# One attention-and-experts kernel: two latencies of its order's planner raised, and all its offsets chosen anew

## The chip, the cores and the metric

The kernel runs on one core of a Trainium2 chip. The metric is the time of one execution on the device in microseconds (us); of several runs the median counts. A span is the time from the first to the last instruction in a profiled execution.

## The reference, cut to what matters

Attention over 8 batches and 8 heads (576 tokens, head size 64) in which each query keeps only its 32 largest scores, and then a layer of 8 experts in which each token, if a skip score is positive, goes to the one expert with the largest gate value.

```python
scores = scale * np.matmul(q, k.transpose(0, 1, 3, 2))
kth = np.partition(scores, -top_k, axis=-1)[..., -top_k:-top_k + 1]      # top_k = 32
scores = np.where(scores >= kth, scores, -1000000000.0)
scores = scores - np.max(scores, axis=-1, keepdims=True)
attn = np.exp(scores)
attn = attn / (np.sum(attn, axis=-1, keepdims=True) + 1e-09)
out = np.matmul(attn, v)
...
do_compute = x @ w_skip > 0
xc = x[do_compute]
logits = xc @ w_gate
e_idx = np.argmax(logits, axis=1)
...
h = np.maximum(xc[mask] @ w1[e], 0.0)            # for each expert e
y[mask] = gate_w[mask, None] * (h @ w2[e])
out[do_compute] = xc + y
```

## The kernel before, in words

**The attention** works on 32 pairs of heads (p = 0 to 31). Each pair has nine rows of 128 queries (`row`, s = 9p + i). For one row TensorE multiplies queries by keys into one of three PSUM row buffers (L652; a first pass with the high parts QH, a second with the low parts QL), VectorE finds the largest values with MAX8 over seven pieces (L662) and narrows them down (L668, L670), ScalarE copies the row out (`xc`, L704) and marks what lies above a bound (`r`, L684), GpSimd multiplies the two (`xw`, L707), VectorE takes the last eight (`wn`, L728), and ScalarE writes the mask PEN (L725). Behind it `unit` multiplies keys by queries once more with the mask added (L867, L869, L874), ScalarE takes the exponential (PT, L899), and `values` multiplies by V and sums up (f1: L950 and L953; f2: L967 and L969; f3 to f9 divide and make the gate's logits).

**What a new pair needs.** `load` brings q and k in (two times three DMAs, L503 and L504), `prep` turns them on TensorE (L537), ScalarE puts the result into TT (L542, L548), GpSimd splits it into high and low parts (HI L562, LO L565), and ten copies from SBUF to SBUF, issued by SyncE (L570), bring the parts to the partitions where they are needed: KK<-HI, QH<-HI, KK<-LO and last QL<-LO. (Pair 0 is built by compute engines in `first`.) The first row of a pair waits for its copies (`ready`). Each pair also sends its rows' maxima from ScalarE's tile `mt` to QL by six small DMAs on SyncE (`maxes`, L825 and L831), fetches V (L516, L519) and stores its results twice (L366, L367). SyncE issues all of them in one queue in order.

**The order** of all this is not written by hand. `Plan` simulates the five engines at build time. Each task has an engine, a duration, a due value (in rows) and predecessors. It is ready at the end of its predecessors, plus their `lag`, plus a wait `WAIT[(from, to)]` (or `WAIT[from]`). `pick` takes, among tasks that are ready first, the one with the lowest due value; LOOK and GAIN allow a more urgent task that is ready a little later, KEEP holds back tasks that would take the last buffer, and TURN adds to the due value of a TensorE task that needs another tile mode (128 or 32 rows). What comes out is only the order in which instructions stand on each engine; on the chip an instruction starts when its semaphores allow, whatever the plan thought. The due values are sums of offsets in `K` and, by row number or part, in `FINE`. A second, shorter plan orders the first expert of the second stage.

**The second stage** (the experts) gathers the tokens of each expert (L1139), runs both matrix products in high and low parts (L1216 to L1218, L1239 to L1241) and scatters the results (L1146). After the first expert its order is fixed by the program text.

Of the kernel before, what the change touches and what calls it, by code (L numbers as in the profile page):

```python
# [25 lines left out]
SKIP = 32  # L26

ENGS = ("PE", "ACT", "DVE", "POOL", "SP")
WAIT = {"PE": 0.2, "ACT": 0.16, ("ACT", "PE"): 0.25, ("ACT", "ACT"): 0.143, "DVE": 0.128, ("DVE", "PE"): 0.25, ("DVE", "POOL"): 0.155, ("ACT", "POOL"): 0.18, "POOL": 0.08, "SP": 0.0,
        ("PE", "PE"): 0.0}  # L30
LOOK, GAIN, KEEP = 0.162, 6.776, 65.356
DRAIN, TURN = 0.2, 29.341
K = dict(qk=-6.401, cand=-6.272, kt=-2.354, push=-12.895, count=-0.049, window=2.533, kth=6.545, rf=32.928, pen=-26.284, u0=6.388, u1=9.914, av=-0.737, a0=3.034, a1=6.191, a2=1.611, co=46.109, sm=-12.508, ca=47.359, tx=-2.868, rt=10.372, rd=-4.654, rs=1.553, pp=12.331, ps=0.569, mx=14.567, f3=5.146, f4=1.248, f5=-7.942, ex=-27.446, us=-0.174, cs=-61.75, ch=0.082, ce=-10.579, lg=1.796, ld=10.949, hl=7.464, hs=-0.126, moe=13.163)

FINE = dict(qk=(-2.911, -0.549, -4.826, -6.903, 2.442, -2.322, -0.945, -1.333, 0.435), ch=(-2.085, -1.45, -1.043, 0.316, -0.011, -0.071, -0.036, -0.392, 1.828), cand=(-3.963, -0.264, 0.827, -1.958, 0.278, 1.229, -5.247, 6.017, 1.231), tx=(-1.055, 5.715, 10.279, 5.202, -1.628, 2.466, 5.022, 2.391, -4.558), kt=(-3.211, 4.865, 0.885, -3.921, -6.437, 3.663, 0.801, 7.673, -4.021), push=(-2.868, -6.928, -2.311, -3.59, 1.547, -1.812, -2.748, -2.193, -12.477), fill=(5.442, -5.764, -1.132, 2.354, -0.665, 2.454, -9.578, 5.161, -6.534), window=(-0.6, 0.433, 0.108, 0.426, -0.223, 0.294, 1.865, -1.999, -0.659), rf=(-2.93, -1.353, -5.81, -2.188, -5.243, -19.285, 10.019, -0.327, -7.401), u=(0.614, -1.895, 0.986, 0.567, -1.265, -0.247, 2.714, -0.285, -0.442), ex=(-1.701, 3.29, -6.117, 0.828, -6.929, -1.417, -0.587, 1.819, -1.658), f1=(-0.189, -4.164, 1.973, -3.388, 0.648, 0.187, -8.021, -2.877, -0.757, -0.71, 1.828, 0.724, -5.471, -2.811, 2.068), f2=(-2.357, -5.603, 1.057, -0.011, -2.434, 5.392, -1.655, -9.716, 1.806), f3=(-2.128, -0.617, 1.736, 2.344, 0.698, -1.856), f4=(3.878, 1.05, -1.924), f5=(3.406, 10.908, 2.309, -4.457, 9.428, 4.705, 2.484, -1.786, 0.821), pp=(-2.088, 3.917, 0.282), pa=(-4.97, -0.526, 1.742), hl=(-0.737, -0.356, 0.256, -2.249), mx=(-1.191, 4.185, 5.019, 0.427, -11.874, -2.914), sm=(-0.212, 0.442, 7.091, 0.24, -3.598, -4.48))
CA = (1, 3, 6, 7)
OUT = (0, 1, 2, 3, 4, 5, 6, 7, 8)
PD = ()
# [7 lines left out]
def tile_kernel(ctx, tc, q, k, v, w_skip, w_gate, w1, w2, out):  # L46
# [7 lines left out]
    REM = S - NM * P  # L54
    assert REM == 64 and D == 64 and H % 4 == 0
    NR = 2 * NM + 1
# [18 lines left out]
    ld = att.enter_context(tc.tile_pool(name="ld", bufs=2))  # L75
# [199 lines left out]
    pl = Plan()  # L275
# [30 lines left out]
    lg = cp.tile([P, B, KC, E + 1], F32, name="lg")  # L306
# [216 lines left out]
    def prep(p):  # L523
        i = p % NQ
        hi, lo = slice(0, D), slice(D, P)

        old = [ROWQ[s] for s in range(NR * (p - NQ), NR * (p - NQ + 1))] + TU[p - NQ] if p >= NQ else []
        TURNED[0, p], TURNED[1, p] = [], []
        puts = {0: [], 1: []}

        def turn(h, blocks):

            def f():
                pm = h()
                for j, (nm, t) in enumerate(blocks):
                    src = RAW[nm][:, t] if t < NM else RAWR
                    nc.tensor.transpose(pm[:, j * P:(j + 1) * P], src.rearrange("p h d -> p (h d)"), identF)  # L537
            return f

        def put(h, nms):  # L540
            if len(nms) == 1:
                nc.scalar.activation(TT[:, nms[0], REM:S], h.t[:, 0:MAIN], AF.Copy)  # L542
            else:

                a = TT[:, :, 0:REM]
                a = bass.AP(a.tensor, a.offset, [a.ap[0], a.ap[1], [S, 2], a.ap[2]])
                src = h.t[:, 0:P].rearrange("p (n c) -> p n c", n=2)
                nc.scalar.activation(a, src[:, :, None, :].to_broadcast([P, 2, 2, REM]), AF.Copy)  # L548
        groups = [[(0, t) for t in range(NM)], [(0, NM)], [(1, t) for t in range(NM)]]
        for j, g in enumerate(groups):  # L550
            nms = [0, 1] if j == 1 else [g[0][0]]
            h = Hold(BT, 1)
            due = NR * p - K["pp"] + K["ps"] * j
            x = pl.add("PE", 0.11 * len(g), due + FINE["pp"][j], turn(h, g), [LOADED[nm, p] for nm in nms], take=h)
            y = pl.add("ACT", 0.478 if len(g) > 1 else 0.265, due + 0.1 + FINE["pa"][j], lambda h=h, nms=nms: put(h, nms), x,
                       [SPLIT[nm, p - 1] for nm in nms] if p else None, give=[h])
            for nm in nms:
                TURNED[nm, p].append(x)
                puts[nm].append(y)

        def high(nm):
            nc.gpsimd.tensor_copy(HI[:, nm], TT[:, nm])  # L562

        def low(nm):
            nc.gpsimd.tensor_tensor(LO[:, nm], TT[:, nm], HI[:, nm], op=OP.subtract)  # L565

        def copy(dst, src):
            if len(dst.shape) == 3:
                src = src[:, None, :].to_broadcast(list(dst.shape))
            nc.sync.dma_start(dst.bitcast(F32), src.bitcast(F32))  # L570
        COPIED[p] = []
        if p == 0:
            first(puts)
            return
        for nm in range(2):
            due = NR * p - K["hl"] + K["hs"] * nm
            x = pl.add("POOL", 0.73, due + FINE["hl"][2 * nm], lambda nm=nm: high(nm), puts[nm], CFREE.get(nm))
            y = SPLIT[nm, p] = pl.add("POOL", 1.57, due + FINE["hl"][2 * nm + 1], lambda nm=nm: low(nm), x)
            c = []
            for h in range(2):  # L580

                ps, cs, ds = slice(h * D, (h + 1) * D), slice(REM * (1 - h), S + REM * (1 - h)), slice(HB * h, HB * h + S)
                of_hi, of_lo = HI[ps, nm, cs], LO[ps, nm, cs]
                for dst, src, z in ((KK[i][hi, :, ds], of_hi, x), (KH[i][lo, ds], of_lo, y)) if nm == 0 else (
                        (QH[i][hi, ds], of_hi, x), (QH[i][lo, ds], of_hi, x), (QL[i][hi, ds], of_lo, y)):
                    c.append(pl.add("SP", 0.67, NR * p - 3 + h, lambda dst=dst, src=src: copy(dst, src), z, old, lag=2.4))
            CFREE[nm] = c
            COPIED[p] += c
        if old:
            COPIED[p].append(pl.add("SP", 0.67, NR * p - 3, lambda: copy(QL[i][D:D + 2], QL[i][D + 2:D + 4]), old, lag=2.0))  # L590
# [311 lines left out]
    def heads(p):  # L902
# [30 lines left out]
        def values(pair, n, hs, due, at):  # L933

            h = Hold(VB, 2)
            st = {}
            z = n == REM
# [18 lines left out]
            def f2(kcs):  # L956

                for kc in kcs:
                    for u, (a, qs) in enumerate(pair):
                        for t in range(1 if z else n // P):  # L960
                            r0 = 64 * u + 32 * (kc % 2 if z else t)
                            o = h.t[r0:r0 + 32, 256:256 + m]
                            first = kc < SA + (2 if z else 1)
                            cs = slice(qs + t * P, qs + t * P + m)
                            if kc < NM:
                                pt = pts[a][:, kc, cs] if kc > SA or not SA else SUM[2 * p + a][:, cs]
                                nc.tensor.matmul(o, ones, pt, start=first, stop=(kc > NM - 2 and z), tile_position=(0, r0))  # L967
                            else:
                                nc.tensor.matmul(o, oneh[:, a], pr[:, cs], start=first, stop=True, tile_position=(0, r0))  # L969
# [53 lines left out]
            A = pl.add  # L1023
# [6 lines left out]
            us = users[:]  # L1030
            for j in range((NM + 2 - SA) // 2):
                kcs = range(SA + 2 * j, min(SA + 2 * j + 2, KC))
                y = A("PE", 0.45 if n > REM else 0.235, due + K["av"] * (2 + 2 * j) + FINE["f2"][3 * at + j], lambda kcs=kcs: f2(kcs), us[-1],
                      [SUMMED[2 * p + a] for a in hs], mode=32)
                us.append(y)
            due += K["av"] * KC + K["f3"]
# [7 lines left out]
            y = A("DVE", 0.11, due + K["f5"] + FINE["f5"][3 * at + 1], f8, x, LGFREE[-3:-2], give=[h4])  # L1044
# [35 lines left out]
    y = pl.add("SP", 5.0, 18.0, load_gate, x, lag=2.5)  # L1080
# [511 lines left out]
```

## Time and profile before

| what | value |
|---|---|
| median of 3 runs | 1198.71 us (1194.42 to 1203.68) |
| the profiled execution's own time | 1204.32 us |
| its span | 1202.4 us |
| TensorE (PE) busy | 1120.5 us, 93% |
| VectorE (DVE) busy | 998.4 us, 83% |
| ScalarE (ACT) busy | 935.2 us, 78% |
| GpSimd (POOL) busy | 749.0 us, 62% |
| mean granted TensorE clock | 0.973 |

The profile lists how long each engine was busy and what ended each of its idle times. Shares over the whole span mix two stages: the attention, up to about 880 us, and the experts after it. PE's busy time is modelled, so a busy PE may still work slowly; the column PEclk (1.00 is 2.4 GHz, 0.50 is 1.2 GHz) tells when.

### The profile page before, as it was taken

The page shows a single profiled execution, that of the slowest core. Times are in us where ns is not written, and L with a number is a line of the kernel's source. Part 1 is how long each engine was busy: PE and PEld are TensorE (multiplying, and loading weights), DVE is VectorE, ACT ScalarE, POOL GpSimd, SP SyncE. Part 2 cuts the span into 40 slices and gives each one's busy share as a digit, 9 for nine tenths or more (in the row PEclk, how much of TensorE's full clock was granted, in tenths as well). Part 3 has the DMA queues.
Part 4 walks back from the last instruction along what each step waited for, and adds up shares of the span by engine and source line. Part 5 has one row for each costly group of instructions (what it writes and reads, how often), then busy time and mean ns, then how long its engine had stood idle before and what let it go on. Part 6 is the DMA issues. An engine that isn't in the chain of part 4 may idle for free. (4 is left out here: it accounts for less than half of the span.)

```text
span 1202.4 us, 37703 instructions
## 1 busy us (share of the span) xinstructions
PE 1120.5 (93%) x13012; PEld 947.2 (79%) x13012; DVE 998.4 (83%) x5250; ACT 935.2 (78%) x1965; POOL 749.0 (62%) x997
## 2 busy tenths in 40 slices
PE   4899999999999999999999999999988999999996
PEld 3778888778778788888887788877767988888885
DVE  8899999989899899999999999999965655655541
ACT  5899999989899899999998799998962533333320
POOL 7778787767777688777877799877842022222210
PEclk9699999989999999999998899999989999999998
DMA  6445455545454455654545354753056554544300
GB/s 146 94 111 119 112 131 133 131 116 131 114 121 112 112 127 136 146 131 125 121 110 130 82 120 117 165 151 84 22 178 188 164 166 155 162 160 155 113 21 25
DMA packets 197404, 148.42 MB, mean 123 GB/s; under 512 B 100898, under 2 KB 162850, under 8 KB 197204
## 3 DMA queue, kind: packets, MB, share of 16 engines
q1 hardware_dynamic: 190340, 135.54, 44.5%
q0 software_dynamic: 3840, 9.47, 2.3%
q8 instruction: 105, 1.72, 0.6%
q10 hardware_dynamic: 3024, 0.90, 0.3%
q14 instruction: 95, 0.78, 0.2%
HBM read 68.31 MB, written 25.31 MB: 78 GB/s over the span
## 5 line engine op out<-in xcount | busy, mean ns | idle before, releaser
L707 POOL TENSOR_TENSOR xw<-xc,r 128x576 f32<-128x576 f32 x288 | 369.9, 1285 | 158.3 <-ACT r L684 153.9
L662 DVE MAX8 cand<-r 128x8 f32<-128x82 f32 (+1 forms) x2016 | 384.4, 235 | 20.8 <-PE r L652 20.5
L684 ACT ACTIVATE r<-xc,cl 128x576 bf16<-128x576 f32 x288 | 223.6, 777 | 23.4 <-DVE cl L668 19.1
L725 ACT ACTIVATE PEN<-xc,wn 128x576 bf16<-128x576 f32 x288 | 222.5, 774 | 1.8 <-DVE wn L728 1.6
L728 DVE MAX8 wn<-xw 128x8 f32<-128x585 f32 x288 | 216.8, 753 | 0.8 <-POOL xw L707 0.7
L867 PE MATMUL r<-QH,KK 128*128 128x256 f32 (+1 forms) x640 | 190.9, 325 | 5.8 <-ACT PT L899 3.6
L704 ACT ACTIVATE xc<-r 128x576 f32<-128x576 f32 x288 | 184.9, 642 | 8.1 <-DVE cand L662 6.6
L869 PE MATMUL r<-QL,KK 66*128 66x256 f32 (+1 forms) x640 | 175.1, 301 | 0.4 <-DMA QL<-mt 0.4
L652 PE MATMUL r<-KK,QH 128*128 128x288 f32 x640 | 160.7, 342 | 13.2 <-ACT xc L704 5.7
L668 DVE MAX8 cl<-cand 128x8 f32<-128x28 f32 (+2 forms) x864 | 166.6, 193 | 4.4
L899 ACT ACTIVATE PT<-r 128x576 f32<-128x576 f32 x256 | 162.9, 645 | 6.3 <-PE r L874 6.0
L1146 POOL DMA_INDIRECT out_dram<-ot,idx x24 | 24.4, 1018 | 214.4 <-DVE ot L1145 167.2
L652 PE MATMUL r<-KK,QL 66*128 66x288 f32 x640 | 137.8, 306 | 18.2 <-DMA QL<-LO 16.3
L1112 DVE TENSOR_TENSOR lo<-raw,hi 128x1024 fp32r<-128x1024 f32 x64 | 79.1, 1238 | 76.4 <-ACT hi L1109 75.5
L867 PEld LDWEIGHTS r<-QH,KK 128*128 128x128 f32 x640 | 120.5, 194 | 19.5 <-ACT PT L899 7.8
L874 PE MATMUL r<-nbi,PEN 128*128 128x128 bf16 (+1 forms) x1632 | 133.3, 217 | 0.0
L1109 ACT ACTIVATE hi<-raw 128x1024 fp32r<-128x1024 f32 x64 | 67.4, 1055 | 75.9 <-PE py L1241 71.4
L652 PEld LDWEIGHTS r<-KK,QL 66*128 66x128 f32 x640 | 104.9, 196 | 21.3 <-issue 10.8
L869 PEld LDWEIGHTS r<-QL,KK 66*128 66x128 f32 x640 | 120.7, 194 | 0.7 <-issue 0.7
L652 PEld LDWEIGHTS r<-KK,QH 128*128 128x128 f32 x640 | 98.4, 196 | 28.8 <-ACT xc L704 7.7
L670 DVE MATCH_REPLACE8 cand<-cl,cand 128x28 f32<-128x28 f32 x576 | 103.4, 180 | 0.0
L1221 ACT ACTIVATE hh<-ph 128x352 fp32r<-128x352 f32 (+2 forms) x72 | 30.9, 431 | 91.1 <-PE ph L1218 89.3
(256 smaller groups left out, 2574.0 us busy)
## 6 DMA issues: line engine op xcount, KB each, us to landing
raw<-in_moe_w_dram SPq DMA_DIRECT2D x64, 512.0 KB
KK<-HI SPq DMA_DIRECT2D x62, 288.0 KB
QH<-HI SPq DMA_DIRECT2D x124, 144.0 KB
QL<-LO SPq DMA_DIRECT2D x62, 144.0 KB
KK<-LO SPq DMA_DIRECT2D x62, 144.0 KB
raw<-in_k_dram SPq DMA_DIRECT2D x64, 128.0 KB
V<-in_v_dram SPq DMA_DIRECT2D x32, 256.0 KB
raw<-in_q_dram SPq DMA_DIRECT2D x62, 128.0 KB
```

The costliest lines, as they stand in the source:

```text
L652: nc.tensor.matmul(R(u, w), t[0:k0, c:c + P], KH[i2][0:k0, HB * hd + u:HB * hd + w], start=(k0 == P and x == 0), stop=(k0 < P and x == len ...
L662: nc.vector.max(C[s][:, c], R(CH[c], CH[c + 1]))
L668: nc.vector.max(L[:, 4 * r:4 * r + 8], c)
L684: nc.scalar.activation(RR[s], XC[s], AF.Sign, bias=CL[p][:, i, 23:24], scale=-ODD, accum_out=CN[:, s:s + 1])
L704: nc.scalar.activation(XC[s], R(), AF.Copy)
L707: nc.gpsimd.tensor_tensor(xw()[:, 0:S], XC[s], RR[s], op=OP.mult)
L725: nc.scalar.activation(pen, XC[s], AF.Relu, bias=least, scale=-1.0)
L728: nc.vector.max(WN[p][:, i], XW[s] if out_ else R())
L867: nc.tensor.matmul(t, KH[i2][:, ks], QH[i2][:, qs], start=(y == 0), stop=False)
L869: nc.tensor.matmul(t, KO[i2][:, ks], QL[i2][0:D + 2, qs], start=False, stop=False)
L874: nc.tensor.matmul(rb[:, O + c:O + c + z - a], PEN[p][:, PS * i + REM + c0 - o:PS * i + REM + c0 - o + P], nbi[:, a:z], start=False, stop= ...
L899: return pl.add("ACT", 0.535, due + K["ex"] + FINE["ex"][at], lambda: nc.scalar.activation(dst, st["r"], AF.Exp, scale=scale), x, give=[h])
```

## The change

Three things are edited in the planner's inputs; no instruction is added or taken out.

1. `WAIT` gets an entry ("ACT", "SP"): 1.2. Before, SyncE's tasks after ScalarE fell back on `WAIT["ACT"]`, 0.16.
2. The ten copies between partitions in `prep` get lag 3.0 where they had 2.4.
3. The duration of f2's tasks is written as a product with the number of blocks. With SA = 1 there are two blocks in each, so 0.45 stays 0.45, and 0.235 becomes 0.236.
4. LOOK, GAIN, KEEP, TURN and all values of `K` and `FINE` are replaced.

```diff
-WAIT = {"PE": 0.2, "ACT": 0.16, ("ACT", "PE"): 0.25, ("ACT", "ACT"): 0.143, ..., ("ACT", "POOL"): 0.18, "POOL": 0.08, "SP": 0.0,
+WAIT = {"PE": 0.2, "ACT": 0.16, ("ACT", "PE"): 0.25, ("ACT", "ACT"): 0.143, ..., ("ACT", "POOL"): 0.18, ("ACT", "SP"): 1.2, "POOL": 0.08, "SP": 0.0,
-LOOK, GAIN, KEEP = 0.162, 6.776, 65.356
-DRAIN, TURN = 0.2, 29.341
-K = dict(qk=-6.401, cand=-6.272, kt=-2.354, push=-12.895, ..., rf=32.928, ..., sm=-12.508, ..., mx=14.567, ..., cs=-61.75, ..., ld=10.949, hl=7.464, ..., moe=13.163)
+LOOK, GAIN, KEEP = 0.164, 7.176, 67.94
+DRAIN, TURN = 0.2, 39.21
+K = dict(qk=-6.436, cand=-7.822, kt=-6.355, push=-12.756, ..., rf=40.955, ..., sm=-27.744, ..., mx=16.505, ..., cs=-44.193, ..., ld=11.234, hl=6.901, ..., moe=22.067)
-FINE = dict(qk=(-2.911, -0.549, -4.826, ...
+FINE = dict(qk=(-2.582, -5.481, -3.89, ...
...
-                    c.append(pl.add("SP", 0.67, NR * p - 3 + h, lambda dst=dst, src=src: copy(dst, src), z, old, lag=2.4))
+                    c.append(pl.add("SP", 0.67, NR * p - 3 + h, lambda dst=dst, src=src: copy(dst, src), z, old, lag=3.0))
...
-                y = A("PE", 0.45 if n > REM else 0.235, due + K["av"] * (2 + 2 * j) + FINE["f2"][3 * at + j], lambda kcs=kcs: f2(kcs), us[-1],
+                y = A("PE", (0.225 if n > REM else 0.118) * len(kcs), due + K["av"] * (2 + 2 * j) + FINE["f2"][3 * at + j], lambda kcs=kcs: f2(kcs), us[-1],
```

## Rows read from the trace of the kernel before

**Rows 1.** Busy time by stretch, whole span in parts: us, busy us (instructions), clock, DMA

```profile
0.00:40.00 40.00, 20.93 (x90) 17.45 (x91) 35.03 (x172) 26.16 (x51) 30.34 (x70) 0.84 0.58 134
...
880.00:900.00 20.00, 15.82 (x268) 13.49 (x271) 9.25 (x21) 12.60 (x23) 8.88 (x12) 0.86 0.79 251
900.00:1000.00 100.00, 93.55 (x648) 83.60 (x639) 56.70 (x116) 38.93 (x66) 19.97 (x33) 0.99 0.53 170
```

**Rows 2.** The same view, the attention in pieces (columns PE, PEld, DVE, ACT, POOL)

```profile
60.00:228.00 168.00, 161.30 (x2257) 134.26 (x2259) 162.59 (x989) 164.15 (x362) 129.98 (x166) 1.00 0.50 119
228.00:256.00 28.00, 25.36 (x324) 20.52 (x313) 22.88 (x140) 23.76 (x53) 20.23 (x26) 0.88 0.51 118
256.00:284.00 28.00, 27.24 (x390) 22.88 (x392) 27.19 (x167) 27.33 (x61) 20.41 (x26) 1.00 0.50 119
284.00:312.00 28.00, 25.60 (x343) 21.41 (x336) 24.22 (x151) 24.67 (x55) 20.43 (x26) 0.94 0.50 119
312.00:396.00 84.00, 81.71 (x1199) 68.64 (x1198) 81.39 (x500) 82.84 (x185) 66.42 (x83) 1.00 0.53 127
396.00:424.00 28.00, 25.21 (x309) 20.49 (x312) 23.77 (x146) 24.23 (x54) 19.01 (x26) 0.94 0.46 109
424.00:620.00 196.00, 190.53 (x2705) 159.48 (x2698) 191.26 (x1156) 191.54 (x424) 154.20 (x198) 1.00 0.56 134
620.00:676.00 56.00, 52.68 (x646) 43.54 (x649) 52.14 (x286) 46.75 (x101) 38.15 (x48) 0.88 0.47 111
```

**Rows 3.** DVE's and PE's waits, 40 to 880 us: total us, times, longest us

```profile
DVE cand L662 <- PE r L652: 20.5, 24, 2.5
PE r L652 <- DMA QL<-LO: 16.3, 10, 2.8
```

**Rows 4.** DVE's waits again, of the stretches 226:257, 283:311 and 390:420

```profile
DVE cand L662 <- PE r L652: 4.6, 2, 2.5
DVE cand L662 <- PE r L652: 3.3, 2, 1.7
DVE cand L662 <- PE r L652: 3.8, 2, 2.2
```

**Rows 5.** Timeline around 248 us: start us, us, engine line op, idle before

```profile
247.56 1.16 SPq L570 DMA_DIRECT2D QL<-LO  x2
...
249.99 0.85 PE L652 MATMUL r<-KK,QL 66*128 66x288 f32 x2 [2.65 <-DMA QL<-LO]
...
250.77 3.64 PE L950 MATMUL pt<-PT,V 128*32 128x256 f32 x32
250.88 0.25 DVE L662 MAX8 cand<-r 128x8 f32<-128x83 f32 x1 [2.08 <-PE r L652]
```

**Rows 6.** Busy time by stretch of 1.5 us around that wait

```profile
247.50:249.00 1.50, 0.00 (x0) 0.00 (x0) 1.29 (x7) 1.50 (x5) 1.24 (x2) 1.00 0.18 43
249.00:250.50 1.50, 0.51 (x2) 0.50 (x2) 0.00 (x0) 0.85 (x2) 0.36 (x3) 0.62 0.71 162
250.50:252.00 1.50, 1.50 (x14) 0.60 (x16) 1.12 (x9) 0.08 (x1) 0.00 (x0) 0.50 0.00 0
```

**Rows 7.** Timeline of SyncE's queue ahead of it, 238 to 247 us

```profile
238.41 0.62 SPq L516 DMA_DIRECT2D V<-in_v_dram  x1
...
240.51 0.62 SPq L366 DMA_DIRECT2D xd<-xb  x1
...
241.86 2.11 SPq L366 DMA_DIRECT2D out_dram<-xb  x1
...
244.75 2.72 SPq L831 DMA_DIRECT2D QL<-mt  x4
```

**Rows 8.** Timeline around 146 us: ScalarE's `mt` and SyncE's issue behind it

```profile
145.71 0.25 ACT L825 ACTIVATE mt<-pa 8x128 fp32r<-8x128 f32 x1
...
145.98 1.23 SPq L831 DMA_DIRECT2D QL<-mt  x2
```

More of the change, by code (lines that the diff above doesn't have):

```diff
@@ L28 @@
 ENGS = ("PE", "ACT", "DVE", "POOL", "SP")
-WAIT = {"PE": 0.2, "ACT": 0.16, ("ACT", "PE"): 0.25, ("ACT", "ACT"): 0.143, "DVE": 0.128, ("DVE", "PE"): 0.25, ("DVE", "POOL"): 0.155, ("ACT", "POOL"): 0.18, "POOL": 0.08, "SP": 0.0,
+WAIT = {"PE": 0.2, "ACT": 0.16, ("ACT", "PE"): 0.25, ("ACT", "ACT"): 0.143, "DVE": 0.128, ("DVE", "PE"): 0.25, ("DVE", "POOL"): 0.155, ("ACT", "POOL"): 0.18, ("ACT", "SP"): 1.2, "POOL": 0.08, "SP": 0.0,
         ("PE", "PE"): 0.0}
-LOOK, GAIN, KEEP = 0.162, 6.776, 65.356
@@ L32 @@
-DRAIN, TURN = 0.2, 29.341
-K = dict(qk=-6.401, cand=-6.272, kt=-2.354, push=-12.895, count=-0.049, window=2.533, kth=6.545, rf=32.928, pen=-26.284, u0=6.388, u1=9.914, av=-0.737, a0=3.034, a1=6.191, a2=1.611, co=46.109, sm=-12.508, ca=47.359, tx=-2.868, rt=10.372, rd=-4.654, rs=1.553, pp=12.331, ps=0.569, mx=14.567, f3=5.146, f4=1.248, f5=-7.942, ex=-27.446, us=-0.174, cs=-61.75, ch=0.082, ce=-10.579, lg=1.796, ld=10.949, hl=7.464, hs=-0.126, moe=13.163)
-FINE = dict(qk=(-2.911, -0.549, -4.826, -6.903, 2.442, -2.322, -0.945, -1.333, 0.435), ch=(-2.085, -1.45, -1.043, 0.316, -0.011, -0.071, -0.036, -0.392, 1.828), cand=(-3.963, -0.264, 0.827, -1.958, 0.278, 1.229, -5.247, 6.017, 1.231), tx=(-1.055, 5.715, 10.279, 5.202, -1.628, 2.466, 5.022, 2.391, -4.558), kt=(-3.211, 4.865, 0.885, -3.921, -6.437, 3.663, 0.801, 7.673, -4.021), push=(-2.868, -6.928, -2.311, -3.59, 1.547, -1.812, -2.748, -2.193, -12.477), fill=(5.442, -5.764, -1.132, 2.354, -0.665, 2.454, -9.578, 5.161, -6.534), window=(-0.6, 0.433, 0.108, 0.426, -0.223, 0.294, 1.865, -1.999, -0.659), rf=(-2.93, -1.353, -5.81, -2.188, -5.243, -19.285, 10.019, -0.327, -7.401), u=(0.614, -1.895, 0.986, 0.567, -1.265, -0.247, 2.714, -0.285, -0.442), ex=(-1.701, 3.29, -6.117, 0.828, -6.929, -1.417, -0.587, 1.819, -1.658), f1=(-0.189, -4.164, 1.973, -3.388, 0.648, 0.187, -8.021, -2.877, -0.757, -0.71, 1.828, 0.724, -5.471, -2.811, 2.068), f2=(-2.357, -5.603, 1.057, -0.011, -2.434, 5.392, -1.655, -9.716, 1.806), f3=(-2.128, -0.617, 1.736, 2.344, 0.698, -1.856), f4=(3.878, 1.05, -1.924), f5=(3.406, 10.908, 2.309, -4.457, 9.428, 4.705, 2.484, -1.786, 0.821), pp=(-2.088, 3.917, 0.282), pa=(-4.97, -0.526, 1.742), hl=(-0.737, -0.356, 0.256, -2.249), mx=(-1.191, 4.185, 5.019, 0.427, -11.874, -2.914), sm=(-0.212, 0.442, 7.091, 0.24, -3.598, -4.48))
@@ new lines @@
+LOOK, GAIN, KEEP = 0.164, 7.176, 67.94
+DRAIN, TURN = 0.2, 39.21
+K = dict(qk=-6.436, cand=-7.822, kt=-6.355, push=-12.756, count=2.92, window=2.675, kth=4.11, rf=40.955, pen=-24.387, u0=6.301, u1=10.019, av=-0.812, a0=2.517, a1=7.268, a2=2.062, co=45.04, sm=-27.744, ca=48.91, tx=-2.41, rt=9.211, rd=-4.985, rs=1.779, pp=12.011, ps=0.546, mx=16.505, f3=5.424, f4=2.403, f5=-9.516, ex=-28.018, us=-0.294, cs=-44.193, ch=0.074, ce=-10.653, lg=3.943, ld=11.234, hl=6.901, hs=-0.757, moe=22.067)
+FINE = dict(qk=(-2.582, -5.481, -3.89, -8.634, 2.584, 2.127, -10.311, -0.581, 0.84), ch=(-1.795, -2.353, 0.375, 0.793, 0.148, 0.584, 0.691, 0.077, 1.361), cand=(-1.518, 3.009, -2.854, 2.234, 3.794, 8.314, -13.849, 8.733, -4.444), tx=(-7.309, 8.112, 10.895, -0.436, -3.418, 2.251, 3.006, 2.193, -6.819), kt=(1.199, -5.41, 3.207, 0.09, -13.647, 9.823, 2.073, 6.692, -9.627), push=(-0.971, 1.213, -8.601, -7.217, -7.838, -8.591, -16.897, -6.494, -17.066), fill=(-1.311, -13.37, -0.279, 9.655, -10.804, 4.889, -2.212, 4.578, -11.905), window=(0.819, 1.021, 0.718, 0.966, -3.002, 0.554, 1.232, -1.806, -0.198), rf=(-22.522, 10.634, 1.224, -3.592, 6.048, -19.969, 16.131, 5.46, -7.455), u=(0.431, -2.113, 3.07, -0.83, -1.126, -0.262, 2.084, 0.0, -0.252), ex=(-0.268, 3.873, -7.012, 5.017, -7.539, -6.305, 3.208, 1.062, 9.247), f1=(-0.307, -7.829, 0.531, -11.444, 3.552, 0.808, -8.16, -5.429, -2.231, -1.171, 3.027, -7.096, -2.147, 0.528, 3.354), f2=(2.824, -9.163, -2.735, 0.994, 1.385, 2.745, 0.885, -26.583, -5.384), f3=(1.313, -8.125, 5.01, 3.389, -6.819, -10.277), f4=(0.229, -1.199, 1.516), f5=(-1.634, 12.144, 9.987, 3.507, 11.997, -6.327, 2.63, -4.211, 2.937), pp=(-0.09, 1.953, -0.174), pa=(0.186, 0.421, 4.08), hl=(-2.048, -1.268, 0.128, -0.999), mx=(1.431, 7.366, 5.928, 5.863, -25.882, -4.637), sm=(-3.276, -4.91, 12.852, -0.333, -10.098, 5.904))
```

## The prediction

> **What bounds the kernel now.** I read the time by stretch first. From 900 us on PE is busy 93.55 of 100 us and VectorE 56.70 [rows 1]; that stage's order, after its first expert, is fixed by the text and the change does not touch it. The attention is another matter: in its undisturbed pieces VectorE and ScalarE are busy nearly all the time. The four pieces with clock 1.00 before 620 us (60 to 228, 256 to 284, 312 to 396, 424 to 620) add up to 462.4 us of VectorE's work in 476 us, 97.1%, or 27.2 of each 28 us [rows 2]. So the attention runs at VectorE's pace, and time can be won only where VectorE stands idle.
>
> Next I read VectorE's waits. Nearly all of its idle time that has an owner is one line: the first MAX8 of a row waits for the row's matmuls, 20.5 us in 24 times; PE in turn waits 16.3 us in 10 times for the copy QL<-LO, at the front of a new pair [rows 3]. Three of these waits are long, and there the clock falls as well: the pieces around 248, 304 and 411 us have a mean clock of 0.88, 0.94 and 0.94, and VectorE does 22.88, 24.22 and 23.77 us of work where 27.2 are usual [rows 2]. The timeline of the first shows the chain: QL<-LO is issued from 247.56 us on, PE stands still 2.65 us until 249.99, VectorE 2.08 us until 250.88 [rows 5]; PE did nothing from 247.5 to 249, and after that its clock is 0.50, the lower level of 1.2 GHz [rows 6].
>
> Last I read SyncE's queue ahead of that copy: V, two stores and four sends of maxima, without a pause, from 238.41 to 247.47 us [rows 7]. The plan has 7.38 us for these (2.0 for V, two times 1.35 for the stores, four times 0.67); the chip took 9.15 us up to the issue of QL<-LO at 247.56, 1.8 us more. On the other side the plan believed this pair of copies landed 3.74 us after the first issue (two times 0.67 and lag 2.4), and PE went on 2.43 us after it [rows 5]. The plan's errors have both signs, and the sum came out late.
>
> **The change part by part.** No instruction is added or removed: the same matmuls, VectorE instructions and DMAs run, so no term is a price of an operation. What changes is the order.
>
> (1) ScalarE to SyncE, 0.16 to 1.2. The trace gives the true figure: `mt` ends at 145.96 us and SyncE's issue begins at 145.98 us [rows 8], 0.02 us. The new value is a safety margin, not a better measurement. It concerns the sends of maxima, which stand at the head of SyncE's burst for each pair or in front of QL<-LO. With 1.04 us more, the plan can put loads ahead of a send and believes that all behind it comes later.
>
> (2) The copies' lag, 2.4 to 3.0. Again a margin for the copy that binds (3.74 planned against 2.43 seen, both from above), yet it works against SyncE's lag of 1.8 us, which the plan still does not know. Both edits together make the front of a pair look up to 1.64 us later. The ten waits are 16.3/10 = 1.63 us long on average [rows 3]: the size fits what PE should be told. The plan then puts other TensorE work (the value products, the second score products) ahead of the new pair's first row, or has the loads and splits earlier.
>
> A rule of the Trainium skill speaks against (2): its page DMA: Bandwidth & Descriptors (Anatomy of one DMA) gives one DMA a fixed cost of about 2.0 us, nearly all of it until the write is acknowledged. The trace is near it with 2.43 us for two issues; by both, 2.4 was already enough after the issue and 3.0 is too much. What follows if that decides is the second rival.
>
> (3) The f2 durations move by at most 0.001 us a task: nothing, from both sides.
>
> (4) The offsets. They cost nothing in themselves; which order comes out of them can't be worked out by hand. Some say where work goes: TURN from 29.3 to 39.2 rows holds TensorE longer in one tile mode, `ld` brings loads 0.29 rows earlier, `hl` the splits 0.56 rows later, `mx` the maxima 1.9 rows earlier, `sm` GpSimd's sums 15 rows earlier. I bound them by what idle time there is: below by nothing gained, above by the waits that rows show.
>
> The sum, against the profiled execution (1204.3 us):
> - the three long waits and their slow clock: (27.2 - 22.88) + (27.2 - 24.22) + (27.2 - 23.77) = 10.7 us [rows 2]. I take all of it, since waits of that length are what a shift of 1.64 us removes; bounds 0 and 10.7.
> - the shorter waits: of VectorE's 20.5 us, 4.6 + 3.3 + 3.8 = 11.7 lie in the stretches of the three [rows 3, 4]; of the other 8.8 us I take half, 4.4, because where no other work is ready the order can't help; bounds 0 and 8.8.
> - the two falls of the clock from 620 to 676 us (27.2 of 28 against 52.14 of 56, 2.3 us) come where another plan can lose as easily as win [rows 2]: 0, bounds 0 and 2.3.
> - prologue and handover: PE is busy 20.93 of the first 40 us and 15.82 of 20 us around 890 [rows 1]. New order, sign unknown: 0, bounds 7 either way, about a third of 19.1 us, an estimate.
>
> That is 15.1 us: 1189.2 us as an execution of the profiled one's kind. That execution was 5.6 us above the median of the runs; taken from the median itself the sum gives 1183.6. If the falls of the clock come and go, the median holds fewer of them. I take the middle, 1186.
>
> On the price of a fall the skill's page TensorE: Matmul & The Clock Gate (Terms) has a rule: time at half rate costs half of itself. The trace fits in kind: around 250.5 us the clock is 0.50 with PE busy throughout [rows 6]. As the term above is taken from VectorE's missing work, it does not use that rule.
>
> **The rivals.**
>
> *Hidden anyway.* The copies land when SyncE gets to them, and the queue is full ahead of QL<-LO [rows 7]. PE is then busy with other work instead of standing still, its clock stays up, but VectorE still has no row. For it: VectorE's waits of 2.08 us at 250.88 follow the landing alone [rows 5]. Against: with three row buffers earlier rows can carry VectorE over. Only the slow-clock part is won: 10.7 less the longest single waits of the three stretches, 2.5 + 1.7 + 2.2 [rows 4], is 4.3 us: 1194.
>
> *Over-caution, slower than before.* Place: the first row of a pair on PE. Only 10 waits are there for 31 pairs with copies, so about 21 pairs had their copies in time. There the plan now believes up to 1.64 us too much and may put value products in front of a row that could run; one burst of 32 such matmuls took 3.64 us, at the low clock [rows 5]. Where row buffers run empty VectorE pays. It decides from 12/21 = 0.57 us a pair; at half of 1.64 us it is 17.2 us, less the 4.3 us of clock: 1212. This is also what the DMA page's rule comes to. Against it: VectorE's waits are rare in the undisturbed pieces, so rows are usually ahead of it.
>
> *All waits gone.* The new offsets were chosen together and remove the short waits and the later falls too: 10.7 + 8.8 + 2.3 = 21.8 us: 1177. Against it: the waits are few and in different places, and any order makes some.
>
> *Nothing done*: the first two edits change no order by themselves at pairs where nothing competes. As other offsets come with them, that case is within the hidden one.
>
> **How the numbers follow.** Forecast (1179 to 1193, the second bound where the short waits stay and the median already lacks a fall) 0.42; hidden 0.25; over-caution 0.15; all waits gone 0.18. The predicted time is 1186. Low: all waits gone and the prologue's 7 us as well, 1170. High: the bound between hidden and full over-caution, 1194 + 13, 1207, which leaves out some 0.1 above and less below. A measurement of this kernel tells about 1% from no change: faster means under 1186.7. Just over half of the forecast and all of the last case lie there: 0.42. Slower (over 1210.7) takes most of the over-caution and a little for offsets that fit the chip badly: 0.14. The rest, 0.44, is within 1%.
>
> **What the changed profile would show.** If right: the ten waits of PE for QL<-LO have shrunk below 5 us in sum, the pieces between 228 and 424 us have clock 1.00 and VectorE at 27 of 28 us, and the attention's last rows come some 15 us earlier. If hidden: PE's wait is gone, VectorE's wait for the row matmuls still near 20 us. If over-cautious: PE's waits for copies gone, VectorE's wait for rows well over 20 us while PE is in value products. Wrong altogether it would be if a new owner of idle time came up on VectorE (GpSimd's product or ScalarE's mark), or if the prologue or the handover moved by more than 10 us.

## The result

The changed kernel takes 1182.34 us (median of 4 runs, 1181.03 to 1183.34) against 1197.87 us of the kernel before in the same sets (1194.42 to 1203.68): a ratio of 0.9865, 95% interval 0.9824 to 0.9905, 15.5 us less. In a later set the same kernel took 1181.86 us (ratio 0.9854, 0.9825 to 0.9883). The forecast was 1186 us, in a range of 1170 to 1207. The profiled execution has a span of 1180.3 us, 22.1 us under the 1202.4 us of before; some 6 us of these are that the profiled execution of before was above its own median.

Busy time by stretch, the changed kernel, the same stretches as [rows 1, 2] (us; PE, PEld, DVE, ACT, POOL busy; clock; DMA):

```profile
60.00:228.00 168.00, 165.96 (x2331) 137.81 (x2331) 165.70 (x1005) 166.35 (x369) 135.38 (x170) 1.00 0.53 128
228.00:256.00 28.00, 27.73 (x374) 23.32 (x375) 27.66 (x169) 27.76 (x62) 22.50 (x32) 1.00 0.55 131
...
284.00:312.00 28.00, 27.82 (x385) 23.26 (x387) 27.66 (x169) 27.76 (x63) 21.82 (x29) 1.00 0.54 135
...
396.00:424.00 28.00, 27.85 (x395) 23.03 (x398) 27.66 (x168) 27.76 (x62) 22.79 (x29) 1.00 0.49 121
424.00:620.00 196.00, 192.03 (x2685) 160.27 (x2678) 193.35 (x1155) 191.29 (x422) 155.33 (x199) 0.99 0.55 131
620.00:676.00 56.00, 53.04 (x712) 44.59 (x711) 54.34 (x314) 49.89 (x110) 42.72 (x57) 0.94 0.44 106
880.00:900.00 20.00, 15.62 (x106) 13.56 (x106) 14.00 (x52) 6.99 (x13) 4.23 (x17) 0.91 0.80 260
900.00:1000.00 100.00, 97.22 (x572) 88.12 (x572) 54.60 (x92) 40.15 (x61) 18.43 (x16) 1.00 0.51 164
```

The three pieces that had a mean clock of 0.88, 0.94 and 0.94 have 1.00, and VectorE works 27.66 of 28 us in each, where it worked 22.88 to 24.22 and where 27.2 was the best that [rows 2] showed on average. VectorE's and PE's longest waits between 40 and 870 us, beside [rows 3]:

```profile
DVE sm L998 <- PE pa L990: 3.5, 1, 3.5
DVE xw L716 <- ACT r L684: 3.2, 10, 0.5
DVE cand L662 <- PE r L652: 2.9, 4, 1.0
...
PE r L867 <- ACT PT L899: 4.5, 7, 1.7
PE r L652 <- ACT xc L704: 4.2, 4, 2.2
```

VectorE waits 2.9 us for a row's matmuls, not 20.5, and no wait of PE for QL<-LO is left of the 16.3 us. The 3.5 us at the top are one single wait that was not there before. SyncE's queue over one pair (start us, us):

```profile
191.81 1.30 SPq L503 DMA_DIRECT2D raw<-in_k_dram  x2
...
195.96 1.48 SPq L570 DMA_DIRECT2D KK<-HI  x1
197.87 1.32 SPq L831 DMA_DIRECT2D QL<-mt  x2
199.29 1.18 SPq L570 DMA_DIRECT2D QH<-HI  x2
200.57 0.54 SPq L570 DMA_DIRECT2D QL<-LO  x1
...
205.55 0.65 SPq L570 DMA_DIRECT2D QL<-LO  x1
206.25 0.61 SPq L570 DMA_DIRECT2D KK<-LO  x1
206.96 0.53 SPq L516 DMA_DIRECT2D V<-in_v_dram  x1
...
208.82 0.62 SPq L366 DMA_DIRECT2D xd<-xb  x1
...
211.54 2.73 SPq L831 DMA_DIRECT2D QL<-mt  x4
```

The copies now stand ahead of V, of the stores and of the four sends; in [rows 5, 7] QL<-LO was behind all of them. The loads stand ahead of the two sends, where before two sends stood first [rows 8].

The trace also tells how early the copies are. Each pair has 20 matmuls with QH in L652 and ten copies in L570, so the first row of pair p and the landings of its copies (the last update of each copy's semaphore that the trace holds) can be counted off. **Slack** below is the time from the last landing of a pair's copies to the first matmul of its first row. Before, it was negative in all 13 pairs from 6 to 18 (-1.0 to -3.7 us): the row's first pass had begun, and in 12 of the 13 PE then stood idle for 0.6 to 2.8 us ahead of the second, 18.2 us in all; at pair 12, with -1.0 us, it did not. The pairs of the kernel before line up by their slack: with -1.0 us a pair takes 25.4 us, with -1.7 to -2.8 us 25.8 to 26.9, and with -3.1, -3.5 and -3.7 us, where the clock falls too, 29.0, 29.4 and 30.5. In the changed kernel the slack is 6.9 to 10.1 us. The span, cut at first rows (one execution of each kernel):

| kernel | first row of pair 6 at us | pair 6 to 18, us (a pair) | pair 18 to 31 | rest | span | slack in pairs 6 to 18 |
|---|---|---|---|---|---|---|
| before | 167.5 | 324.9 (27.07) | 359.1 | 350.9 | 1202.4 | -3.7 to -1.0 |
| changed | 165.6 | 308.9 (25.74) | 352.1 | 353.7 | 1180.3 | 6.9 to 10.1 |
| e1 | 167.6 | 305.4 (25.45) | 357.6 | 350.1 | 1180.7 | -1.1 to 1.5 |
| e2 | 165.8 | 308.9 (25.74) | 352.1 | 353.9 | 1180.6 | 1.0 to 3.8 |
| e3 | 174.7 | 304.4 (25.37) | 358.7 | 349.2 | 1187.0 | -0.4 to 2.1 |
| e4 | 177.8 | 310.7 (25.89) | 349.6 | 353.8 | 1191.8 | 7.0 to 9.5 |
| e5 | 168.7 | 311.1 (25.92) | 357.0 | 353.0 | 1189.9 | -2.1 to 0.8 |
| e6 | 174.7 | 304.4 (25.37) | 359.3 | 355.7 | 1194.1 | 0.8 to 2.0 |
| e7 | 171.2 | 313.3 (26.11) | 360.3 | 348.2 | 1193.0 | -0.7 to 13.4 |
| e8 | 164.8 | 308.7 (25.72) | 349.4 | 355.5 | 1178.4 | 6.8 to 10.0 |

Of the 22.1 us, 16.0 come from pairs 6 to 18, 7.0 from pairs 18 to 31, 1.9 from the start, and 2.8 are lost behind the last pair's first row. Late copies can account for little beyond the first of these: outside pairs 6 to 18 PE did not stand idle between the two passes of a first row in the kernel before either.

### The profile page after: what moved, and what is told of

It reads as the page before. It is cut to its first block, busy times and chain, and to the rows that moved or that the text cites. A ratio compares the mean times of both kernels' runs of the same rounds, so it can differ in the third digit from the quotient of the medians.

```text
span 1180.3 us, 37612 instructions
## 1 busy us (share of the span) xinstructions
PE 1117.7 (95%) x13012; PEld 947.0 (80%) x13012; DVE 1000.2 (85%) x5250; ACT 931.8 (79%) x1965; POOL 752.6 (64%) x997
## 5 line engine op out<-in xcount | busy, mean ns | idle before, releaser
L662 DVE MAX8 cand<-r 128x8 f32<-128x82 f32 (+1 forms) x2016 | 366.7, 234 | 3.0 <-PE r L652 2.9
L684 ACT ACTIVATE r<-xc,cl 128x576 bf16<-128x576 f32 x288 | 224.8, 780 | 16.3 <-DVE cl L668 15.3
L867 PE MATMUL r<-QH,KK 128*128 128x256 f32 (+1 forms) x640 | 190.3, 324 | 10.1 <-ACT PT L899 4.5
L704 ACT ACTIVATE xc<-r 128x576 f32<-128x576 f32 x288 | 188.6, 655 | 9.5 <-DVE cand L662 3.9
L652 PE MATMUL r<-KK,QH 128*128 128x288 f32 x640 | 162.2, 344 | 14.0 <-ACT xc L704 6.6
L899 ACT ACTIVATE PT<-r 128x576 f32<-128x576 f32 x256 | 166.9, 654 | 3.1 <-PE r L874 2.9
L652 PE MATMUL r<-KK,QL 66*128 66x288 f32 x640 | 135.1, 302 | 0.0
L652 PEld LDWEIGHTS r<-KK,QH 128*128 128x128 f32 x640 | 98.2, 196 | 41.0 <-ACT PT L899 12.2
L652 PEld LDWEIGHTS r<-KK,QL 66*128 66x128 f32 x640 | 103.9, 194 | 0.3 <-issue 0.3
```

The lines of the kernel that those rows point to most:

```text
L652: nc.tensor.matmul(R(u, w), t[0:k0, c:c + P], KH[i2][0:k0, HB * hd + u:HB * hd + w], start=(k0 == P and x == 0), stop=(k0 < P and x == len ...
L662: nc.vector.max(C[s][:, c], R(CH[c], CH[c + 1]))
L684: nc.scalar.activation(RR[s], XC[s], AF.Sign, bias=CL[p][:, i, 23:24], scale=-ODD, accum_out=CN[:, s:s + 1])
L704: nc.scalar.activation(XC[s], R(), AF.Copy)
L867: nc.tensor.matmul(t, KH[i2][:, ks], QH[i2][:, qs], start=(y == 0), stop=False)
L899: return pl.add("ACT", 0.535, due + K["ex"] + FINE["ex"][at], lambda: nc.scalar.activation(dst, st["r"], AF.Exp, scale=scale), x, give=[h])
```

## The experiments

Theory A: SyncE issued QL<-LO too late, and that alone cost the time. Theory B: the new order on the compute engines made the gain. The first two experiments move entries of SyncE's queue and leave the order on every other engine as it was.

**e1: the kernel before, with V and the stores behind QL<-LO.** The plan is unchanged; only the moment at which a SyncE task is written out is.

In the extract below `LOWS` counts the copies QL<-LO of the next pair that are still to come, and `flush` writes out what is held.

```diff
+    def emit(x):
...
+        if x.tag in ("v", "store") and LOWS[0]:
+            HELD.append(x)
+            return
+        x.f()
+        if x.tag == "low":
+            LOWS[0] = (LOWS[0] or 2) - 1
+            if not LOWS[0]:
+                flush()
...
-                    x.f()
+                    emit(x)
```

> The kernel before, with one thing moved: in SyncE's queue the V loads and the stores of a pair go behind QL<-LO of the next pair instead of ahead of it; the order on all other engines stays. Theory A (the place of the copies in SyncE's queue is what cost the time): the copies land some 6 us earlier, PE's waits for QL<-LO fall from 16 us to under 2, the clock falls at 248, 304 and 411 us are gone, a pair in the steady stretch takes 25.6 to 25.9 us, and the time is 10 to 18 us under before, about 1183. Theory B (the order on the compute engines made the gain): only the three long waits go, 3 to 8 us are won, about 1192, and a pair still takes 26.2 to 26.5 us.

Measured: 1179.99 us, ratio to before 0.9861 (0.9814 to 0.9908). The timeline of SyncE, e1 (where [rows 7] had V and stores):

```profile
237.02 2.69 SPq L859 DMA_DIRECT2D QL<-mt  x4
239.82 1.16 SPq L595 DMA_DIRECT2D QL<-LO  x2
241.02 0.58 SPq L540 DMA_DIRECT2D V<-in_v_dram  x1
...
242.89 0.64 SPq L390 DMA_DIRECT2D xd<-xb  x1
```

VectorE's wait for the rows in e1, 40 to 870 us (the line numbers have moved with the edit):

```profile
DVE cand L689 <- PE r L679: 3.3, 4, 1.9
```

No wait of PE for QL<-LO is left, a pair takes 25.4 us in the steady stretch, and the three falls of the clock are gone. Theory A holds in this direction: moving three groups of issues within one queue wins as much time as the whole change. Theory B's 1192 us does not. Two things differ from what A expected. The copies were to come some 6 us earlier, and the slack grew by 1.5 to 4.6 us only; in three of the 13 pairs it is still -0.8 to -1.1 us, and yet PE stands idle for no more than 0.1 us there. And the time is not won in the same places: e1 wins 19.5 us in pairs 6 to 18 and 1.5 behind them up to pair 31, the changed kernel 16.0 and 7.0. So these 7.0 us are the new order's, and in that part theory B has a share.

**e2: the changed kernel, with QL<-LO behind V, stores and sends.**

The copies QL<-LO carry the tag `low`, the four sends of a pair's first five rows the tag `send`:

```diff
+    def emit(x):
...
+        if x.tag == "low":
+            HELD.append(x)
+            return
+        x.f()
+        if x.tag == "send" and HELD:
+            SENT[0] += 1
+            if SENT[0] == 4:
+                flush()
...
-                    x.f()
+                    emit(x)
```

> The changed kernel, with one thing moved: QL<-LO goes behind the V loads, the stores and the four sends of maxima in SyncE's queue, where it stood before; the order on all other engines is that of the changed kernel. Theory A: the copies lose 9 to 10 us, all of the slack that they have ahead of the next pair's first row; PE's waits for QL<-LO come back and the time rises by 5 to 18 us, to about 1193. Theory B: the new order on the compute engines holds the gain: at most 3 us more, about 1184.

Measured: 1182.09 us, ratio to before 0.9889 (0.9844 to 0.9934), the same as the changed kernel. Taken alone this is what B expected. The slack shows why it isn't evidence for B: the copies lost about 7 us, not 9 to 10, and still landed 1.0 to 3.8 us ahead of the first rows.

```profile
209.34 2.72 SPq L859 DMA_DIRECT2D QL<-mt  x4
212.11 1.16 SPq L595 DMA_DIRECT2D QL<-LO  x2
```

The first row that needs these comes at 217 us. So the experiment did not go far enough, and e5 goes on from it.

**e5: as e2, with five small DMAs (4 KB each) ahead of each pair's QL<-LO.** `pause` issues them, from an SBUF tile to scratch tiles in DRAM; beside e2 the edit adds:

```diff
             if SENT[0] == 4:
+                pause()
                 flush()
```

> The changed kernel with QL<-LO behind the sends of maxima as in e2, and five small DMAs of SyncE (4 KB to a scratch tile, some 3.1 us together) ahead of each pair's QL<-LO. In e2 the copies still landed 1.0 to 2.5 us ahead of the next pair's first row in the steady stretch, and no time was lost. Theory A (only a landing behind the first row costs): the copies now land 0.5 to 2.5 us too late, PE's waits for QL<-LO come back in 10 or more pairs, the clock falls in some of them, a pair takes 26 to 27 us instead of 25.6, and the time is 12 to 30 us over the changed kernel. Theory B (the compute engines' order carries the gain whatever the copies do): within 5 us of the changed kernel.

Measured: 1190.59 us, ratio to before 0.9914 (0.9891 to 0.9938); 8.5 us over e2 (the kernel before came out at 1196.45 us in the set of e2 and at 1200.07 in that of e5, the changed kernel at 1181.86 to 1182.34 in its two sets, and e8's kernel, in e5's set and in a later one, at 1179.53 and 1178.95, so the times themselves are compared here). PE's waits and SyncE's queue in e5:

```profile
PE r L687 <- DMA QL<-LO: 7.0, 7, 2.0
```

```profile
265.59 3.42 SPq L204 DMA_DIRECT2D scratch<-wi  x5
269.05 1.17 SPq L603 DMA_DIRECT2D QL<-LO  x2
```

With 3.42 us more the slack in pairs 6 to 18 is -2.1 to 0.8 us and the waits are back. They are smaller than A had expected: 7 in place of 10 or more, a pair takes 25.92 us in place of 26 to 27, and the 8.5 us lie under A's 12 to 30 and over B's 5. Where e2's 7 us cost nothing, the next 3.4 us cost 8.5 us of time. That is a threshold at the first row, as A says, but one at a slack of about -1 us and not at zero: the pairs of e5 at -1.0 us or above lose nothing at their first row. The trace accounts for the loss. Of the 9.3 us between the spans of e2 and e5 only 2.2 lie in pairs 6 to 18; 3.0 lie ahead of them and 4.9 in pairs 18 to 31, where the slack goes down to -3.1 us (0.9 is won behind). Over all pairs PE stands idle for 9.3 us between the two passes of first rows, in e2 for 0.0. The five DMAs also lengthen SyncE's queue for the loads behind them; this sum leaves little for that.

**e3, e6, e7: the margins on the old offsets**, both of them (e3), the wait alone (e6), the lag alone (e7).

The first two lines are the edit of e3 and e6, the last two that of e3 and e7 (lines cut at both ends):

```diff
-... ("ACT", "POOL"): 0.18, "POOL": 0.08, ...
+... ("ACT", "POOL"): 0.18, ("ACT", "SP"): 1.2, "POOL": 0.08, ...
-... z, old, lag=2.4))
+... z, old, lag=3.0))
```

> The kernel before with the two margins (wait 1.2 and lag 3.0) and all old offsets. Theory A1 (the margins move the copies): the plan sees copies late, puts loads ahead of the sends, PE's waits for QL<-LO fall under 6 us, and the time is 6 to 14 us under before, 1184 to 1192. Theory A2 (margins alone only give another order; the new offsets are what places the copies early): between 5 us under and 10 us over before, 1193 to 1208, with other waits in place of the old.

> The kernel before with the wait from ScalarE to SyncE at 1.2 and nothing else. In e3 both margins on the old offsets brought the copies 1 to 2 us ahead of the first rows and a pair to 25.3 us. Theory W (the wait does it, since with the new offsets the lag leaves the order as it is): the same here, a pair takes 25.3 to 25.6 us, 1185 to 1193. Theory L (the lag does it): copies late as before, a pair 26.3 us or more, 1194 to 1202.

> The kernel before with the copies' lag at 3.0 and nothing else. Theory W: copies as late as before, a pair takes 26.3 us or more, 1194 to 1202. Theory L: copies in time, a pair 25.3 to 25.6 us, 1185 to 1193.

Measured: e3 1189.61 us (ratio 0.994, 0.9916 to 0.9965); e6 1193.65 us (0.9941, 0.9919 to 0.9964); e7 1194.84 us (0.9962, 0.9944 to 0.998). SyncE's queue in e3:

```profile
244.22 0.62 SPq L366 DMA_DIRECT2D xd<-xb  x1
...
245.62 2.07 SPq L570 DMA_DIRECT2D QL<-LO  x2
247.78 2.69 SPq L831 DMA_DIRECT2D QL<-mt  x4
250.52 0.65 SPq L366 DMA_DIRECT2D out_dram<-xb  x1
```

With the wait at 1.2 the plan puts QL<-LO ahead of the sends and of the second store, and that is enough: a pair takes 25.37 us in e3 and e6, less than in the changed kernel. So e3 came out as A1 expected, in its time and in its waits. e3 and e6 lose some of it elsewhere: the first row of pair 6 comes at 174.7 us where it came at 167.5, so the re-planned start costs 7 us. Theory W named the mechanism rightly, and e6's time lies 0.7 us above its range. The lag alone (e7) also brings most copies in time, with slack up to 13.4 us, so theory L's first half holds too; but a pair takes 26.11 us, and why is not settled.

In the changed kernel the lag does nothing at all. Built with 2.4 in place of 3.0 its instructions stand in the same order on all five engines; there is no run of it.

**e4: the changed kernel with the wait back at 0.16.**

> The changed kernel with the wait from ScalarE to SyncE back at 0.16; lag 3.0 and all new offsets kept. Theory A1 (the margin is needed): sends go back in front of the loads, waits for copies come back, 8 to 16 us over the changed kernel, 1190 to 1198. Theory A2 (the offsets carry the gain): copies keep their slack, within 5 us of the changed kernel, 1178 to 1187.

Measured: 1192.99 us, ratio 0.9971 (0.9948 to 0.9993). The time is the one of A1, but its reason is wrong. The copies keep their slack (7.0 to 9.5 us), as A2 said, and a pair takes 25.89 us. So the new offsets bring the copies in time without the wait, and without the new offsets the wait does so too, and the lag for most of them. The loss lies at the start, where pair 6 begins 12.2 us later than in the changed kernel, and pair 3 already 8.8 us later (97.5 against 88.7 us). Busy time from 60 to 100 us, first the changed kernel, then e4, and PE's longest wait of e4 in it:

```profile
60.00:100.00 40.00, 38.81 (x551) 31.20 (x552) 39.42 (x242) 39.57 (x89) 33.44 (x40) 1.00 0.52 123
```

```profile
60.00:100.00 40.00, 32.72 (x362) 26.34 (x360) 31.77 (x188) 33.25 (x70) 27.59 (x32) 0.79 0.43 100
```

```profile
PE r L652 <- ACT xc L704: 5.1, 4, 2.3
```

PE waited in this stretch 5.1 us in 4 times for ScalarE's copy of a row, its clock fell to a mean of 0.79, and VectorE did 31.77 us of work in place of 39.42.

**e8, e9, e10: f2's duration back at 0.235** (e8, and again as e10 beside the changed kernel itself as e9).

```diff
-                y = A("PE", (0.225 if n > REM else 0.118) * len(kcs), ...
+                y = A("PE", 0.45 if n > REM else 0.235, ...
```

> The changed kernel with f2's short duration back at 0.235 in place of 0.236. No resource changes. Theory C (a plan so tuned is fragile, and any new order makes its own stumbles at the start and behind pair 20): a pair in the steady stretch still takes 25.6 us and the copies keep their slack, but the sum moves by 3 to 10 us, to 1185 to 1192. Theory D (so small a step does nothing): within 2 us of the changed kernel.

> The changed kernel itself, beside e10 on the same chip, so that the two can be compared within one set of runs. Both theories of e8 expect some 1182 us here.

> The kernel of e8 (f2's short duration at 0.235) beside e9. Theory C (the step of 0.001 us in the plan makes another order, and its place at the start and behind pair 20 is worth some us): 2 to 4 us under e9, with no overlap of the runs. Theory D (what e8 showed was the difference between two sets of runs): within 1 us of e9.

Measured: e8 1179.53 us (ratio 0.9829, 0.9811 to 0.9848); in the second set e9 1181.86 us (1180.61 to 1183.45) and e10 1178.95 us (1178.67 to 1179.66), with no overlap. So the step of 0.001 us in a planned duration makes the kernel 2.9 us slower. Theory C is right in kind, and e10 came out as it said; the sign that e8 had expected is wrong, as undoing the step gains. SyncE's order is the same up to about 640 us; pairs 18 to 31 take 349.4 us in e8 and 348.8 in e10, against 352.1 in the changed kernel and 352.0 in e9. With f2's old duration the kernel beats both: 1178.95 us, 0.9832 of before.

## Why the prediction was right

**The chain was right.** VectorE idle behind a row's matmuls, these behind QL<-LO, that behind V, stores and sends in SyncE's queue: e1 changes only the last link and wins 16.5 us. One reading ahead of it was wrong: VectorE doesn't set the attention's pace alone. In the four pieces of [rows 2] from which its 462.4 us were added up ScalarE has 465.9 of 476 us.

**The long waits: 10.7 us forecast.** The three pairs with falls of the clock went from 30.5, 29.0 and 29.4 us to 25.6 us each in the changed kernel, 12.0 us together, and to 25.4 us in e1, 12.7 us. The term was a little small, as the usual 27.2 of 28 us that it was taken against was itself held down by short waits.

**The short waits: the reason was wrong.** I took half of 8.8 us, because where no other work is ready the order can't help. In the changed kernel VectorE's waits for rows are 2.9 us in all, so most of it came back. The step asked what work could fill the wait; the new plan did not fill it, it had the copies land earlier. The other nine pairs from 6 to 18 won 6.8 us in e1, from 26.2 us each to 25.5, and 4.0 us in the changed kernel, whose order is a little slower once no copy is late. So 4.4 is near the time that was won there, by two errors that cancel.

**Pairs 18 to 31: the term that was missing.** They won 7.0 us. The sum had nothing for them but a part of the short waits and a 0, with 2.3 as its bound, for the falls of the clock behind 620 us. Most of what the sum fell short of, against the profiled execution's own time, lies here: 22.1 us measured, 15.1 added up. Between the medians 15.5 us were won. That 15.1 is so near to them is luck: the terms were read from an execution some 6 us above the median, and were too small by about as much. That 1186 came within 4 us is owed to this and to the middle that I took between the two bases.

**The margins: half right.** The sentence on the wait (the plan puts loads ahead of a send and believes that all behind it comes later) is what e6 and the changed kernel's queue show. That the lag works against SyncE's lag holds for the old offsets, where it alone brings most copies in time (e7); in the changed order it does nothing. The sum of 1.64 us beside a mean wait of 1.63 us, on which I leaned, was a coincidence: the new order left the copies 9 us early, not 1.64.

**f2: wrong.** I wrote that a step of 0.001 us is nothing, from both sides. It is 2.9 us, by e9 and e10: a planned duration has no price of its own, but a planner that breaks near ties makes another order of it.

**Prologue and handover: 0, bounds 7 either way.** Measured, up to the first row of pair 6 and behind that of pair 31: 1.9 us won and 2.8 us lost. In other plans the start alone cost 7.2 us (e3, e6) and 10.3 us (e4) against before, so the bound was too narrow for a re-plan.

**The rivals.** *Hidden anyway* fell: VectorE's wait went with PE's. *Over-caution* fell: VectorE's waits for rows are 2.9 us in all, not over 20. Its count of pairs was near: 12 pairs had a standstill, not 10 (the view puts the two at pairs 17 and 18, 1.3 and 0.6 us, down to VectorE), and 19 had none. But the 12 are all among 13 pairs in a row, each with its copies late; a count over the whole attention hides such a stretch. The page DMA: Bandwidth & Descriptors of the Trainium skill (Anatomy of one DMA) spoke against the lag of 3.0 with its fixed cost of about 2.0 us, which it gives for DMAs that GpSimd issues; here SyncE issues, and in the kernel before a copy took 2.5 us (QL<-LO) to 3.8 us (KK<-HI) in the median from its issue to its last landing. No run shows a cost of that lag. *All waits gone*, 1177, is what became of the waits for copies; the time did not reach it, as a pair then takes 25.6 us, close to the work that ScalarE has for it.

**What bounds the steady stretch now.** Busy time from 200 to 460 us, before, changed, e1 and e3:

```profile
200.00:460.00 260.00, 246.13 (x3439) 205.52 (x3441) 240.44 (x1467) 245.12 (x538) 196.78 (x250) 0.97 0.52 125
```

```profile
200.00:460.00 260.00, 258.02 (x3599) 216.23 (x3589) 256.26 (x1554) 257.52 (x570) 207.37 (x267) 1.00 0.54 131
```

```profile
200.00:460.00 260.00, 258.49 (x3661) 216.99 (x3661) 254.72 (x1568) 259.03 (x576) 210.61 (x266) 1.00 0.55 131
```

```profile
200.00:460.00 260.00, 258.51 (x3660) 216.15 (x3658) 254.84 (x1573) 259.95 (x576) 208.51 (x267) 1.00 0.54 129
```

In e3 ScalarE is busy 259.95 of 260 us: at 25.3 us a pair it is the limit, and not VectorE, which I had named. The changed kernel, with ScalarE at 257.52 and no engine full, stays 0.3 us a pair above that.

**What stays open:** which of the new offsets place the copies early, what the new order does in pairs 18 to 31 to win 7.0 us, why e7's pairs take 26.1 us with copies in time, and what makes a start such as e4's. None of these was tried apart.

## What to carry to other kernels

Ask of a wait for a DMA not only how long it is but what stands ahead of that DMA in its queue: here V loads and stores, which nothing waits for soon, stood ahead of a copy that the next row needed, and moving them alone won as much as re-planning everything. Slack beyond the first use is worth nothing here: 7 us taken out of 9 cost nothing, the next 3.4 us cost 8.5. Look at slack pair by pair, not at the count of waits. And in a planned order judge an edit by the order that comes out, part by part (start, steady stretch, end), since margins and even a thousandth of a microsecond re-plan every part at once.

## What the runs showed that was not expected

The kernel before is less steady than all those with copies in time: its runs in one set range from 1190.39 to 1204.06 us (19 runs), those of the changed kernel from 1180.61 to 1183.45 (6 runs), and e10's from 1178.67 to 1179.66 (6 runs). The standard deviation of one set's runs is 3.1 to 3.7 us for the kernel before, 1.9 to 2.6 for e1, e3 and e6 with a slack near zero, and 0.4 to 1.2 for e2, e4, e8, e9 and e10, most of them with 7 us or more; e7, with 2.0, doesn't fit. It fits that the copies of before land within 4 us of the row that needs them, so that small differences decide whether PE stops and its clock falls from 2.4 to 1.2 GHz; that the spread comes from there is argued and was not measured run by run.
